# A fused attention and two expert layers: the first attention in a fixed order, other weights kept on chip, other buffers for coded weights

## The chip, the cores and the metric

The kernel runs on one core of a Trainium2 chip. The core has a matrix engine (TensorE, in the profile PE for products and PEld for the loading of weights), a vector engine (VectorE, DVE), a scalar engine (ScalarE, ACT), a general engine (GpSimd, POOL) and an engine that issues most of the transfers (SyncE, SP). The engines run side by side, each works through its own queue of instructions in order, and they wait for each other by semaphores. The metric is the device time of one execution in microseconds (us), as a median of runs.

## The reference, cut to what matters

```python
def _attn_ref(q, k, v, s):                       # 2 batches, 8 heads, 576 positions, 64 wide
    scores = q @ k.T / 8
    cum = np.cumsum(np.maximum(s, 0.0), axis=-1)
    bias = -(cum[:, :, :, None] - cum[:, :, None, :])
    scores = np.where(causal, -1e9, scores + np.minimum(bias, 0.0))
    attn = softmax(scores)
    return attn @ v
def _moe_ref(x, w_in, w_out):                    # 1152 tokens, 512 -> 2048 -> 512
    h = x @ w_in
    g = np.where(h > 0.0, h, np.exp(np.minimum(h, 0.0)) - 1.0)
    return g @ w_out
def _moe2_ref(x, domain_probs, w1, w2):          # 4 experts, 512 -> 1024 -> 512
    p = domain_probs / (domain_probs.sum(-1, keepdims=True) + 1e-09)
    for e in range(4):
        out += p[:, e:e + 1] * (np.maximum(x @ w1[e], 0.0) @ w2[e])
```

The attention's result, 1152 rows of 512, goes through the second function (called layer one below) and then through the third (layer two).

## The kernel before, in words

The tokens are taken in three groups: 256, 448 and 448 (`GROUPS`). Group 0 has its attention to itself at the start (`attention_first`); the attention of groups 1 and 2 is cut into small parts that run in the background of the products of the group before (`attention_parts`, called by `background` in `slot`). Layer one of group 0 has 16 units (`up1`, `down1`: four products into `up`, an ELU on ACT and DVE that writes `gt`, four products into `acc0` to `acc3`), layer two of group 0 has 32 (`up2`, `down2`). Groups 1 and 2 have layer one each (`layer1`), and layer two for both together at the end: the joint stage, which forms 7 block products instead of 8 from sums of blocks (`pair_steps`, `p1` to `p7`, `c21`, `c22`).

Layer one of group 0 uses exact 32-bit weights, which come in a coded 64-bit form (`w64`), 512 KB for each half of a unit. `fetch_halves` loads coded halves into whatever buffers are still unused (the list `turn`: tags `gt`, `wu`, `wr`, `cd`, `yh`, `yl`, `raw`, `xa`, `ox`), and `decode_halves` decodes them: ACT takes the magnitude (L158) and, from the fifth half on, the low bits (L165); DVE puts the words together (L166, L168). Twelve decoded units are written back by a transfer of GpSimd's queue (`w_dec`, L171) and loaded again for groups 1 and 2 by `fetch` (L100); the last four stay on chip in the tag `wr` (`kept`, `N_WR`). Weights of the other uses are loaded as they are into `raw` (three buffers) and split into a high and a low part by `prepare` (ACT L106, DVE L87 into `wu`).

`attention_first` has four pairs of heads. For a pair: `scores` (PE L313, L321, L323), `probabilities` (a reduction with mask on DVE, L333, and an exponential on ACT, L335, for each of four blocks), `normalise` (DVE L339 to L344), `transposes` (PE L352, ACT L353), `values` (PE L361, ACT L363). `keep_warm` (L370) multiplies the identity by itself, to no result. `cum_parts`, `cum_columns` and `probabilities_of` prepare operands of the later attention and the expert shares.

What sets the order: a scheduler places the instructions of all engines by estimated times, and `tc.issue_after`, `tc.keep_in_program_order` hold it back where the author wants it. The order on each engine is then fixed. The call for decoding inside the attention is `decode_halves(DEC[i])`; in layer one `advance` calls it with

```python
        decode_halves(min(2 * n + AHEAD, DEC[-1] + 5 * (n + 1) // 2))
```

so that it runs up to ten halves ahead of unit n. The background of group 0 begins at slot 14 of layer one (`BG_FROM`); its first part loads queries, keys and values of the first heads into the tag `pt` (`load_small`, L429), and `split` (L486 to L491) makes `qs`, `qb`, `kh`, `kl` of them on ACT and DVE for `qk` (PE L502, L504).

Of the kernel before, what the change touches and what calls it, by code (L numbers as in the profile page):

```python
# [45 lines left out]
DEC = [1, 2, 3, 4]  # L46
# [4 lines left out]
N_WR, N_WU, N_GT, N_CD = 2, 1, 3, 5  # L51
# [3 lines left out]
def tile_kernel(ctx, tc, qT, kT, v, s, w64, w, probs, out):  # L55
# [39 lines left out]
    def fetch(n):  # L95
        if n >= NU and (n - NU) % NAB in kept:
            fetched[n] = kept[(n - NU) % NAB]
            return
        fetched[n] = t = sb([128, 1024], "raw", 3)
        SP.dma_start(out=t, in_=w[n - NAB] if n < NU else w_dec[(n - NU) % NAB])  # L100

    def prepare(n):
# [9 lines left out]
    small = [("yh", 1, 1), ("yl", 1, 1)] + [("raw", 3, 1)] * 3 + [("xa", 1, 3), ("ox", 1, 3)]  # L112
    turn = ([("gt", 3, 1)] * N_GT + [("wu", 5, 2)] * N_WU + [("wr", N_WR, 2)] * N_WR
            + [("cd", N_CD, 1)] * N_CD + small * 2)
# [9 lines left out]
    n_coded, n_decoded, last_coded = [0], [0], [None]  # L124
# [13 lines left out]

    def decode_halves(upto):

        while n_decoded[0] < min(upto, len(order)):
            i = n_decoded[0]
            n, part = order[i]
            if part == 0:
                if n % 2 == 0:
                    if n < NAB - N_KEPT:
                        pair = sb([128, 2, 1024], "wu", 5)  # L150
                    else:
                        pair = sb([128, 2, 1024], "wr", N_WR)
                        kept[n], kept[n + 1] = pair[:, 0], pair[:, 1]
                    units[n], units[n + 1] = pair[:, 0], pair[:, 1]
            x, m = coded.pop(i), units[n][:, 512 * part:512 * part + 512]
            high, low, mi = x[:, :, 1], x[:, :, 0], m.bitcast(I32)
            tc.keep_in_program_order(
                ACT.activation(m, high.bitcast(F32), AF.Abs, scale=2.0 ** -112))  # L158
            z = sb([128, 512], f"z{i % 2}", 1, I32)
            if i < N_LOW:  # L160
                tc.keep_in_program_order(DVE.tensor_scalar(
                    z, low.bitcast(U32), 7.49 / 2 ** 32, None, op0=ALU.mult))
            else:
                tc.keep_in_program_order(
                    ACT.activation(z, low.bitcast(U32), AF.Copy, scale=7.49 / 2 ** 32))  # L165
            DVE.scalar_tensor_tensor(out=mi, in0=mi, scalar=3, in1=z,  # L166
                                     op0=ALU.logical_shift_left, op1=ALU.bitwise_or)
            DVE.scalar_tensor_tensor(out=mi, in0=high, scalar=-2 ** 31, in1=mi,  # L168
                                     op0=ALU.bitwise_and, op1=ALU.bitwise_or)
            if part and n not in kept:  # L170
                POOL.dma_start(out=w_dec[n], in_=units[n])  # L171
            n_decoded[0] += 1
            fetch_halves()
# [3 lines left out]
    make_identity(nc, ident)  # L177

# [10 lines left out]

    zero = sb([64, 256], "zero", 1)  # L190
    POOL.memset(zero, 0.0)

# [69 lines left out]
    def attention_first(x):  # L265
# [31 lines left out]
        with tc.issue_after(high.ins), tc.issue_after(low.ins):  # L297
            cum_parts()
# [57 lines left out]
        def values(hp):  # L356
            o = ps(f"acc{(hp + 2) % 4}", 1)
# [15 lines left out]
        with tc.issue_after(keep_warm(12).ins):  # L373
            first = scores(0)
            with tc.issue_after(first.ins), tc.issue_after(low.ins):
                cum_columns(0, 4)
                cum_columns(1, 4)
            scores(1)
            scores(2)
        probabilities(0)  # L380
        decode_halves(DEC[0])
        with tc.issue_after(scores(3).ins):
            keep_warm(6)
        probabilities(1)
        with tc.issue_after(normalise(0).ins):
            shares.extend((probabilities_of(0, n // 128), probabilities_of(T2, NCH)))
        with tc.issue_after(transposes(0).ins):
            keep_warm(4)
        probabilities(2)
        normalise(1)  # L390
        transposes(1)
        values(0)
        decode_halves(DEC[1])
        probabilities(3)
# [3 lines left out]
        decode_halves(DEC[2])  # L398
        normalise(3)
        transposes(3)  # L400
        values(2)
        values(3)
        decode_halves(DEC[3])

# [353 lines left out]
    attention_first(x_first)  # L758
    pr_first, pr_later = shares
    xs = [None, None, None]  # L760

    class First:
# [3 lines left out]
        def __call__(self, at):  # L766
            if at > BG_FROM[0]:
                if self.got is None:
                    first_stack.close()
                    att_pool[0] = att_stack.enter_context(  # L770
                        tc.tile_pool(name="att", bufs=1, reuse_waits="tile"))
                    xs[1] = sb([128, 2, NCC, N2], "xa", 1, F32R)
                    self.got = Background(attention_parts(1, xs[1]), BG_FROM[0],
                                          NAB + LAG + E * NCD - BG_TO[0])
# [8 lines left out]
    for c in range(NCC):  # L783
        ACT.activation(yh[:, c], yacc[c], AF.Copy)
        split_lo(yl[:, c], yacc[c], yh[:, c])
    pr = pr_first
# [69 lines left out]
    def pair_steps(q):  # L856
# [3 lines left out]
        def sums():  # L860
            x = raws[q]
            st["t"] = t = l2a.tile([128, 4, 256], F32, tag="sums", name="sums", bufs=1)
# [240 lines left out]
```

## Time and profile before

| what | us |
|---|---|
| median of 3 runs (lowest, highest) | 708.74 (707.78, 709.1) |
| the profiled execution, as a run | 710.54 |
| its span, first to last instruction | 708.4 |
| PE busy, DVE busy, ACT busy, POOL busy in the span | 696.6, 561.7, 382.4, 15.6 |

The profile is one execution. A busy PE is not a PE at its peak: its rows carry the granted clock, 1.00 for 2.4 GHz and 0.50 for 1.2 GHz, and a row of products takes longer at the lower one. Idle time of an engine counts only where the end waits for it, so the timeline of PE and what released each of its waits come first, and from there one goes to the engine or the transfer that was late. A timeline row is: start, duration, engine, line, operation, written tile, read tiles, shapes, count, and in brackets the idle time before it with what ended it. A duration runs to the last write, so the start of the next row on the same engine tells what one instruction costs its queue. Stages of this execution: first attention to 28.3 us, layer one of group 0 to 87, its layer two to about 226, layer one of groups 1 and 2 to 413, the joint stage to the end.

### The profile page before, as it was taken

What the parts mean: (1) busy time and instruction counts of PE and PEld (TensorE: products, weight loads), DVE (VectorE), ACT (ScalarE), POOL (GpSimd) and SP (SyncE); (2) the same over time, 40 slices, a digit from 0 to 9 for tenths busy, and PEclk for the clock granted to TensorE, in tenths of its full rate; (3) what the DMA queues carried; (4) which work ended last, traced back from release to release, by engine and by line L of the source; (5) the groups of instructions that cost most, each with busy time, mean ns of one, the idle gap of its engine ahead of it and who ended that gap; (6) DMA issues with size and microseconds to landing.
All of it is one profiled execution on the core that took longest, in us unless ns stands there. A gap on an engine that the chain in (4) does not pass through costs nothing.

```text
span 708.4 us, 10218 instructions
## 1 busy us (share of the span) xinstructions
PE 696.6 (98%) x3670; PEld 595.6 (84%) x3670; DVE 561.7 (79%) x1146; ACT 382.4 (54%) x773; POOL 15.6 (2%) x36
## 2 busy tenths in 40 slices
PE   8999999999999999999999999999999999999997
PEld 7888788887878887888899988888888888888886
DVE  7799788797868898876975469988888888788765
ACT  5799798786768788866644344322222223332320
POOL 5011000000000000000000000000000000000000
PEclk9899999999999999999999999999999999999999
DMA  8999855655554433113530000111111111111002
GB/s 299 409 368 373 271 174 154 193 166 157 174 185 140 141 125 102 41 47 128 210 140 0 1 1 0 60 60 60 60 61 59 60 60 59 61 60 59 1 0 105
DMA packets 34578, 85.45 MB, mean 121 GB/s; under 512 B 3440, under 2 KB 13888, under 8 KB 34528
## 3 DMA queue, kind: packets, MB, share of 16 engines
q1 hardware_dynamic: 32576, 78.23, 32.7%
q0 software_dynamic: 1952, 6.57, 2.3%
q8 instruction: 29, 0.48, 0.3%
q14 instruction: 21, 0.17, 0.1%
HBM read 75.88 MB, written 8.91 MB: 120 GB/s over the span
## 4 chain that ended last, share of the span: by engine, by line
PE 86%; ACT 7%; DVE 3%; issue 1%; DMA 1%; POOL 0%; SPq 0%; DVEq 0%; ACTq 0%; POOLq 0%
PE acc L626 38%; PE up L626 16%; PE att L938 11%; PE up L938 8%; PE att L581 3%; PE att L554 3%; ACT z L165 2%; ACT wu L158 2%; PE att L509 1%; PE att L502 1%; PE att L504 1%; DMA pt<-in_kT 1%; ACT e L736 1%; PE att L370 1%; PE acc L716 1%
## 5 line engine op out<-in xcount | busy, mean ns | idle before, releaser
L626 PE MATMUL acc<-w,h 128*128 128x512 f32 x672 | 172.0, 392 | 0.0
L626 PEld LDWEIGHTS acc<-w,h 128*128 128x128 f32 x672 | 126.1, 188 | 23.0 <-ACT h L948 0.2
L626 PE MATMUL acc<-gt,wu 128*128 128x448 f32 x384 | 87.8, 372 | 0.0
L948 ACT ACTIVATE h<-c 128x448 fp32r<-128x448 f32 x48 | 27.4, 573 | 111.7 <-DVE c L954 111.7
L683 DVE SCALAR_TENSOR_TENSOR ox<-acc,pr,ox 128x512 f32<-128x512 f32 x105 | 78.6, 748 | 11.1 <-PE acc L626 9.1
L87 DVE TENSOR_TENSOR wu<-raw,wu 128x1024 fp32r<-128x1024 f32 x56 | 68.4, 1223 | 19.5 <-ACT wu L106 17.3
L626 PEld LDWEIGHTS acc<-gt,wu 128*128 128x128 f32 x384 | 70.1, 188 | 7.8 <-issue 2.6
L106 ACT ACTIVATE wu<-raw 128x1024 fp32r<-128x1024 f32 x56 | 59.1, 1055 | 15.8 <-PE acc L626 14.1
L938 PE MATMUL att<-S,top 128*128 128x448 f32 x288 | 66.3, 365 | 0.0
L938 PEld LDWEIGHTS att<-S,top 128*128 128x128 f32 x288 | 54.0, 188 | 6.7 <-issue 0.2
L626 PE MATMUL acc<-wu,gt 128*128 128x512 f32 x192 | 56.8, 411 | 0.0
L626 PE MATMUL up<-yh,wu 128*128 128x256 f32 x256 | 52.5, 287 | 0.0
L949 DVE SCALAR_TENSOR_TENSOR h<-c,h 128x448 fp32r<-128x448 f32 x48 | 29.8, 623 | 18.7 <-ACT h L948 18.7
L938 PE MATMUL up<-x2a,top 128*128 128x448 f32 x192 | 44.2, 366 | 0.0
L626 PEld LDWEIGHTS up<-yh,wu 128*128 128x128 f32 x256 | 41.8, 190 | 2.6 <-issue 1.7
L626 PE MATMUL up<-xa,wu 128*128 128x448 f32 x192 | 43.5, 371 | 0.0
L626 PE MATMUL up<-ox,wu 128*128 128x448 f32 x192 | 41.5, 366 | 0.8 <-DVE e L741 0.8
L544 ACT ACTIVATE p<-p,nm 128x384 f32<-128x384 f32 (+4 forms) x56 | 34.5, 616 | 13.6 <-DVE nm L539 13.2
L948 ACT ACTIVATE h<-up 128x448 fp32r<-128x448 f32 x16 | 8.7, 545 | 59.5 <-PE up L938 59.5
L938 PEld LDWEIGHTS up<-x2a,top 128*128 128x128 f32 x192 | 35.9, 188 | 4.8 <-ACT p L963 0.6
L626 PEld LDWEIGHTS up<-ox,wu 128*128 128x128 f32 x192 | 36.0, 188 | 4.0 <-DVE e L741 1.1
L626 PEld LDWEIGHTS acc<-wu,gt 128*128 128x128 f32 x192 | 32.8, 189 | 6.9 <-issue 2.5
(215 smaller groups left out, 1245.6 us busy)
## 6 DMA issues: line engine op xcount, KB each, us to landing
raw<-in_w SPq DMA_DIRECT2D x38, 512.0 KB
raw<-in_w SPq DMA_DIRECT2D x16, 1024.0 KB
raw<-w_dec SPq DMA_DIRECT2D x24, 512.0 KB
w_dec<-wu POOLq DMA_DIRECT2D x12, 512.0 KB, 7.4
cd<-in_w SPq DMA_DIRECT2D x5, 512.0 KB
xa<-in_w SPq DMA_DIRECT2D x5, 512.0 KB
k<-in_kT SPq DMA_DIRECT2D x8, 288.0 KB
cbp<-cum_d SPq DMA_DIRECT2D x16, 144.0 KB
```

Source lines behind the costliest of these rows:

```text
L87: DVE.tensor_tensor(out=lo, in0=x, in1=hi.bitcast(F32), op=ALU.subtract)
L106: ACT.activation(t[:, 0], x, AF.Copy)
L158: ACT.activation(m, high.bitcast(F32), AF.Abs, scale=2.0 ** -112))
L165: ACT.activation(z, low.bitcast(U32), AF.Copy, scale=7.49 / 2 ** 32))
L544: ACT.activation(p, p, AF.Exp, bias=nm, scale=-1.0, accum_out=sm)
L554: PE.transpose(pt[:cb[c + 1] - cb[c], m, :], p[:, cb[c]:cb[c + 1]], ident)
L581: PE.matmul(o[64 * j:64 * j + 64, qs:nq], job["v"][:n, c, 64 * j:64 * j + 64], job["pt"][:n, j, c, qs:nq], start=c == 0, stop=c == n_c - 1)
L626: PE.matmul(o, a[m], b[n], start=first and i == 0, stop=last and i == 2)
L683: DVE.scalar_tensor_tensor(out=o_sb, in0=o, scalar=pr[:, i, e:e + 1], in1=o_sb, op0=ALU.mult, op1=ALU.add)
L938: PE.matmul(bank, tops[q][:, m, op, cs], x[:, n, c], start=first and c + i == 0, stop=c == 1 and i == 2, skip_group_check=True)
L948: ACT.activation(h[:, 0, u, cs], c, AF.Relu)
L949: DVE.scalar_tensor_tensor(out=h[:, 1, u, cs], in0=c, scalar=0.0, in1=h[:, 0, u, cs].bitcast(F32), op0=ALU.max, op1=ALU.subtract)
```

## The change

The engines PE, ACT and DVE are scheduled by hand inside `attention_first`: the instructions stand in the order in which the function writes them. That order is new: one stretch of eight warm-up products in place of 12, 6 and 4; scores of two pairs, probabilities of two pairs, scores of the other two; the fourth pair's probabilities earlier; decoding not before the fourth `normalise`, save for the magnitude step of two halves (`begin_half`). `cum_columns` and the shares go behind the last decoded word of layer one (`last_word`). The kept units are the first six, not the last four (`N_WR` 3); the `wr` tag holds no coded halves any more, `wu` holds ten of them, `cd` three, twice. Four halves are decoded when the attention ends, as before. The sums of the joint stage go to the tag `xf` for the first two pairs, and to the pool on the right side for the others.

```diff
-DEC = [1, 2, 3, 4]
+DEC = [1, 2, 4]
-N_WR, N_WU, N_GT, N_CD = 2, 1, 3, 5
+N_WR, N_WU, N_GT, N_CD = 3, 5, 0, 3
...
-        SP.dma_start(out=t, in_=w[n - NAB] if n < NU else w_dec[(n - NU) % NAB])
+        SP.dma_start(out=t, in_=w[n - NAB] if n < NU else w_dec[(n - NU) % NAB - N_KEPT])
...
-    small = [("yh", 1, 1), ("yl", 1, 1)] + [("raw", 3, 1)] * 3 + [("xa", 1, 3), ("ox", 1, 3)]
-    turn = ([("gt", 3, 1)] * N_GT + [("wu", 5, 2)] * N_WU + [("wr", N_WR, 2)] * N_WR
-            + [("cd", N_CD, 1)] * N_CD + small * 2)
+    twice = [("cd", N_CD, 1)] * N_CD + [("yh", 1, 1), ("yl", 1, 1)]
+    turn = ([("gt", 3, 1)] * N_GT + [("wu", 5, 2)] * N_WU + twice
+            + [("raw", 3, 1)] * 3 + [("xa", 1, 3), ("ox", 1, 3)] + twice + [("xa", 1, 3)])
...
+    def begin_half(i):
+        n, part = order[i]
+        if part == 0 and n % 2 == 0:
+            if n >= N_KEPT:
+                pair = sb([128, 2, 1024], "wu", 5)
+            else:
+                pair = sb([128, 2, 1024], "wr", N_WR)
+                kept[n], kept[n + 1] = pair[:, 0], pair[:, 1]
+            units[n], units[n + 1] = pair[:, 0], pair[:, 1]
+        begun[i] = m = units[n][:, 512 * part:512 * part + 512]
+        tc.keep_in_program_order(
+            ACT.activation(m, coded[i][:, :, 1].bitcast(F32), AF.Abs, scale=2.0 ** -112))
...
-        with tc.issue_after(high.ins), tc.issue_after(low.ins):
-            cum_parts()
+        cum_parts()
...
-        with tc.issue_after(keep_warm(12).ins):
-            first = scores(0)
-            with tc.issue_after(first.ins), tc.issue_after(low.ins):
-                cum_columns(0, 4)
-                cum_columns(1, 4)
-            scores(1)
-            scores(2)
-        probabilities(0)
-        decode_halves(DEC[0])
-        with tc.issue_after(scores(3).ins):
-            keep_warm(6)
-        probabilities(1)
-        with tc.issue_after(normalise(0).ins):
-            shares.extend((probabilities_of(0, n // 128), probabilities_of(T2, NCH)))
-        with tc.issue_after(transposes(0).ins):
-            keep_warm(4)
+        keep_warm(8)
+        for hp in (0, 1):
+            scores(hp)
+        for hp in (0, 1):
+            probabilities(hp)
+        for hp in (2, 3):
+            scores(hp)
+        normalise(0)
         probabilities(2)
+        transposes(0)
         normalise(1)
+        probabilities(3)
         transposes(1)
+        begin_half(0)
         values(0)
-        decode_halves(DEC[1])
-        probabilities(3)
         normalise(2)
         transposes(2)
         values(1)
-        decode_halves(DEC[2])
+        begin_half(1)
         normalise(3)
+        decode_halves(DEC[0])
         transposes(3)
         values(2)
+        decode_halves(DEC[1])
         values(3)
-        decode_halves(DEC[3])
+        decode_halves(DEC[2])
...
-    attention_first(x_first)
-    pr_first, pr_later = shares
+    with tc.manual_schedule(engines={mybir.EngineType.PE, mybir.EngineType.Activation,
+                                     mybir.EngineType.DVE}):
+        attention_first(x_first)
...
+                    with tc.issue_after(last_word[0].ins):
+                        cum_columns(0, 4)
+                        cum_columns(1, 4)
+                        shares.extend((probabilities_of(0, n_tile), probabilities_of(T2, NCH)))
...
-            st["t"] = t = l2a.tile([128, 4, 256], F32, tag="sums", name="sums", bufs=1)
+            if q < 2:
+                t = sb([128, 4, 256], "xf", 1)
+            else:
+                t = l2b.tile([128, 4, 256], F32, tag="sums", name="sums", bufs=1)
+            st["t"] = t
```

On GpSimd the clearing of `zero` and the first of its two casts (L293 before) move ahead of the masks' selections. Three places show what else the change moves. The lines of the changed kernel are a few numbers off: L352 is L354 there, L361 is L363.

PE between the last scores and the first values of the first attention, before (`k_154` and `k_155` hold the probabilities of the first three heads and of the next three):

```order
L321 MATMUL acc_274<-cump,ones 128x256
L323 MATMUL acc_274<-ones,cumm 128x256
L370 MATMUL att<-ident 128x128 x6
L352 MATMUL att<-ident,k_154 128x128 x6
L370 MATMUL att<-ident 128x128 x4
L352 MATMUL att<-ident,k_154 128x128 x3
L361 MATMUL acc_369<-pt 64x256 x2
```

The same place on PE of the changed kernel:

```order
L323 MATMUL acc_258<-cump,ones 128x256
L325 MATMUL acc_258<-ones,cumm 128x256
L354 MATMUL att<-ident,k_152 128x128 x9
L354 MATMUL att<-ident,k_153 128x128 x3
L363 MATMUL acc_329<-pt 64x256 x2
```

The ten warm-up products between the scores and the values are gone.

SP at the end of decoding, before (`raw` from L135 holds coded halves, from L100 weights of layer two; `pt` are the loads of the background attention):

```order
L135 DMA raw<-in_w 128x1024 x3
L135 DMA xa<-in_w 128x1024 x2
L100 DMA raw<-in_w 128x1024 x3
L429 DMA pt<-in_qT 128x4x128
L429 DMA pt<-in_kT 128x4x128
```

SP of the changed kernel at the same place, and behind it DVE of the changed kernel, where L175 is the last decoded word, L734 the gate `gt`, L231 the columns' copies and L87 the split of weights:

```order
L100 DMA raw<-in_w 128x1024 x3
L135 DMA xa<-in_w 128x1024 x3
L100 DMA raw<-in_w 128x1024 x2
L426 DMA pt<-in_qT 128x4x128
L426 DMA pt<-in_kT 128x4x128
```

```order
L175 SCALAR_TENSOR_TENSOR wu<-xa,wu 128x512 x2
L734 SCALAR_TENSOR_TENSOR gt<-up,e 128x256
L231 COPY cum_782<-cum 16x64 x2
L231 COPY cum_790<-cum 16x64 x2
L259 TENSOR_REDUCE prs<-pr 128x2
L87 TENSOR_TENSOR wu<-raw,wu 128x1024
L260 TENSOR_SCALAR prs<-prs 128x2
L87 TENSOR_TENSOR wu<-raw,wu 128x1024
```

Two more weight loads now stand ahead of the background's first loads; they go into buffers that the two splits (L87) have to free.

ACT at the beginning of the background attention, before (`e` are the exponentials of layer one's units, L733, and their second step, L736):

```order
L486 ACTIVATE qs<-pt 64x512
L733 ACTIVATE e<-up 128x256
L487 ACTIVATE kh<-pt 64x512
L736 ACTIVATE e<-e 128x256
L489 ACTIVATE qb<-pt 64x512
L491 ACTIVATE kh<-pt 64x512
L486 ACTIVATE qs<-pt 64x512
L487 ACTIVATE kh<-pt 64x512
L733 ACTIVATE e<-up 128x256
L491 ACTIVATE kh<-pt 64x512
L736 ACTIVATE e<-e 128x256
```

The same place on ACT of the changed kernel:

```order
L483 ACTIVATE qs<-pt 64x512
L486 ACTIVATE qb<-pt 64x512
L484 ACTIVATE kh<-pt 64x512
L488 ACTIVATE kh<-pt 64x512
L483 ACTIVATE qs<-pt 64x512
L484 ACTIVATE kh<-pt 64x512
L488 ACTIVATE kh<-pt 64x512
L730 ACTIVATE e<-up 128x256
L106 ACTIVATE wu<-raw 128x1024
L733 ACTIVATE e<-e 128x256
```

All seven casts of the first split now stand ahead of the exponential of unit 15, and a cast of weights stands between its two steps. In the joint stage the first two products with the block sum S2 now follow each other on PE, where five products with S3 stood between them, and the four steps of the sums of pair 2 stand among the block sums on DVE.

## Rows read from the trace of the kernel before

**Rows 1.** The page: TensorE's share of the span; traffic of 40 slices.

```profile
PE 696.6 (98%) x3670; PEld 595.6 (84%) x3670; DVE 561.7 (79%) x1146; ACT 382.4 (54%) x773; POOL 15.6 (2%) x36
...
GB/s 299 409 368 373 271 174 154 193 166 157 174 185 140 141 125 102 41 47 128 210 140 0 1 1 0 60 60 60 60 61 59 60 60 59 61 60 59 1 0 105
```

**Rows 2.** Stretches, PE: length, busy time and records, granted clock, transfers' share, GB/s.

```profile
15.10:21.80 6.70, 6.70 (x32) 0.50 1.02 403
21.90:28.00 6.10, 6.10 (x52) 1.00 1.03 421
```

**Rows 3.** Timeline of PE, first attention to the first product of layer two.

```profile
13.98 0.92 PE L313 MATMUL acc<-pt 64*128 64x128 f32 x6 [1.24 <-DVE nm L333]
...
16.56 2.77 PE L370 MATMUL att<-ident 128*128 128x128 f32 x12
19.12 1.49 PE L352 MATMUL att<-ident,k 128*128 128x128 f32 x6
...
27.54 0.87 PE L361 MATMUL acc<-pt 128*64 128x256 f32 x8
...
79.53 0.33 PE L502 MATMUL att<-kh,qs 128*128 128x128 f32 x1 [1.21 <-ACT kh L491]
...
87.04 0.34 PE L626 MATMUL up<-yh,wu 128*128 128x256 f32 x1
```

**Rows 4.** Timeline of DVE in the first attention, and two weight splits later.

```profile
8.00 0.27 DVE L333 CUSTOM_DVE_ANT_0 k<-acc,mask 128x128 f32<-128x128 f32 x1
...
8.55 0.28 DVE L333 CUSTOM_DVE_ANT_0 k<-acc,mask 128x128 f32<-128x128 f32 x1
...
8.96 1.18 DVE L235 COPY cum_p<-cum_t 64x4 f32<-64x4 f32 x4
...
13.84 1.01 DVE L344 TENSOR_SCALAR k<-k,sm 128x128 f32<-128x128 f32 x4
...
74.46 2.36 DVE L87 TENSOR_TENSOR wu<-raw,wu 128x1024 fp32r<-128x1024 f32 x2
```

**Rows 5.** Timeline of ACT: exponentials, first and last decoding steps, casts.

```profile
8.32 0.40 ACT L335 ACTIVATE k<-k,nm 128x128 f32<-128x128 f32 x1 [1.56 <-DVE nm L333]
...
9.21 0.39 ACT L335 ACTIVATE k<-k,nm 128x128 f32<-128x128 f32 x1
...
30.68 0.67 ACT L158 ACTIVATE wu<-wu 128x512 f32<-128x512 f32 x1
...
69.82 0.71 ACT L165 ACTIVATE z<-xa 128x512 int32<-128x512 uint32 x1
71.29 1.06 ACT L106 ACTIVATE wu<-raw 128x1024 fp32r<-128x1024 f32 x1 [0.76 <-DMA raw<-in_w]
...
77.38 0.63 ACT L487 ACTIVATE kh<-pt 64x512 fp32r<-64x512 f32 x1
```

**Rows 6.** Timelines of DVE and POOL, 3 to 5 us: the scan, two casts.

```profile
3.27 1.35 DVE L207 TENSOR_TENSOR_SCAN cum<-bias 16x576 f32<-16x576 f32 x1 [3.27 <-ACT bias L206]
...
3.39 1.43 POOL L293 CAST cump<-zero 64x256 fp32r<-64x256 f32 x1
4.77 0.39 POOL L293 CAST cumm<-zero 64x256 fp32r<-64x256 f32 x1
```

**Rows 7.** Timelines of SP and ACT: the load of s and its use; the queries' load.

```profile
0.75 0.39 SPq L270 DMA_DIRECT2D bias<-in_s  x1
...
2.56 0.68 ACT L206 ACTIVATE bias<-bias 16x576 f32<-16x576 f32 x1 [0.52 <-DMA bias<-in_s]
...
70.01 0.38 SPq L429 DMA_DIRECT2D pt<-in_qT  x1
```

**Rows 8.** The chain that ended last: start, length, what; the keys' load.

```profile
70.44 6.92 DMA pt<-in_kT
```

**Rows 9.** Timelines of DVE and PE, joint stage: S2's low part, its first use.

```profile
421.17 1.08 DVE L87 TENSOR_TENSOR S<-ssum,S 128x896 fp32r<-128x896 f32 x1
...
422.53 0.37 PE L938 MATMUL up<-S,top 128*128 128x448 f32 x1
```

More of the change, by code (lines that the diff above doesn't have):

```diff
@@ L123, in tile_kernel @@
         last_in[tag][-1] = i
-    n_coded, n_decoded, last_coded = [0], [0], [None]
+    n_coded, n_decoded, last_coded, last_word = [0], [0], [None], [None]
     def fetch_halves(upto=len(order)):
@@ L137, in fetch_halves @@
             n_coded[0] += 1
+    begun = {}
+    def begin_half(i):
[10 more added lines that the diff above has]
+            ACT.activation(m, coded[i][:, :, 1].bitcast(F32), AF.Abs, scale=2.0 ** -112))
     def decode_halves(upto):
@@ L146, in decode_halves @@
             n, part = order[i]
[L147 to L155, printed above, removed]
+            if i not in begun:
+                begin_half(i)
+            x, m = coded.pop(i), begun.pop(i)
             high, low, mi = x[:, :, 1], x[:, :, 0], m.bitcast(I32)
-            tc.keep_in_program_order(
-                ACT.activation(m, high.bitcast(F32), AF.Abs, scale=2.0 ** -112))
             z = sb([128, 512], f"z{i % 2}", 1, I32)
@@ L167, in decode_halves @@
                                      op0=ALU.logical_shift_left, op1=ALU.bitwise_or)
-            DVE.scalar_tensor_tensor(out=mi, in0=high, scalar=-2 ** 31, in1=mi,
-                                     op0=ALU.bitwise_and, op1=ALU.bitwise_or)
+            last_word[0] = DVE.scalar_tensor_tensor(out=mi, in0=high, scalar=-2 ** 31, in1=mi,
+                                                    op0=ALU.bitwise_and, op1=ALU.bitwise_or)
             if part and n not in kept:
-                POOL.dma_start(out=w_dec[n], in_=units[n])
+                POOL.dma_start(out=w_dec[n - N_KEPT], in_=units[n])
             n_decoded[0] += 1
@@ L177, in tile_kernel @@
     make_identity(nc, ident)
+    zero = sb([64, 256], "zero", 1)
+    POOL.memset(zero, 0.0)
     mask = sb([128, S], "mask", 1)
@@ L188, in tile_kernel @@
                            pattern=[[-1, 64]], channel_multiplier=1)
-    zero = sb([64, 256], "zero", 1)
-    POOL.memset(zero, 0.0)
     cum = sb([B * H, S], "cum", 1)
@@ L356, in values @@
         def values(hp):
-            o = ps(f"acc{(hp + 2) % 4}", 1)
+            o = ps(f"acc{hp}", 1)
             for c, q0 in ((0, 0), (1, 128)):
@@ L785, in tile_kernel @@
         split_lo(yl[:, c], yacc[c], yh[:, c])
+    pr_first, pr_later = shares
     pr = pr_first
```

## The prediction

> **What bounds the kernel now.** I read the share of each engine on the page first [rows 1]: TensorE is busy 98% of the span, so all that can be won is about 12 us of idle TensorE and the products that do nothing or run at the low clock. The table by stretches puts the latter in front: the granted clock is 0.50 (1.2 GHz) for 6.8 us, from 15.0 to 21.9, and 1.00 (2.4 GHz) again behind that [rows 2]. The timeline of TensorE shows why that stage is long [rows 3]: after a wait of 1.24 us for a reduction of DVE the clock fell, twelve records of the warm-up helper then took 2.77 us at 16.56, and the first transposes came only at 19.12. The last value product starts at 27.54; from there layer one of group 0 is paced by TensorE with one later wait worth naming, 1.21 us at 79.53, for a cast of keys that a load released. Layer two begins at 87.04. What happens before 87.04 is therefore the place to cost; behind it TensorE has hardly any wait to give back.
>
> **The change, part by part.** I make the sum against the profiled execution (span 708.4 us, 710.54 us as a run, so 2.1 us around the span) and carry the difference over to the median of the runs shown, 708.74 us, which is 1.8 us below that execution.
>
> *The start.* GpSimd's first cast took 1.43 us and its twin 0.39; the first stood beside the scan of DVE, which ran from 3.27 to 4.6 [rows 6]. Now the first cast stands ahead of the scan, but the mask's selections and the second cast fall beside it. Freed wholly, the first reduction comes at about 7.35 us (the two splits of the row sums, 1.4 us, from 5.95); held as the first cast was, near the 8.00 of before [rows 4]. I take 7.9, nearer to the row. [...]
>
> *The attention stage.* DVE no longer has the columns' copies there (the four small ones alone 1.18 us [rows 4]), nor the shares, nor any decoding before the fourth normalise; TensorE no longer has the ten products between scores and transposes. What is left is a chain of two engines. A head's two reductions take 0.55 us (8.00 to 8.55), so a pair 1.1; normalising a pair takes four multiplies, 1.01, and two small steps, 1.4 in all [rows 4]; a head's two exponentials take 0.89 (8.32 to 9.21), so a pair 1.78 [rows 5]. From 7.9 DVE needs 4 x 1.1 + 4 x 1.4 = 10.0 us, and about 0.7 us more because the first normalise waits for the first pair's exponentials: 18.6. Behind it come the last transposes (0.8), their two evictions queued on ACT behind the first mantissa step of the decoder (about 1.9 in all), so the last value product starts at 21.3 instead of 27.54 [rows 3]: 6.2 us earlier.
>
> *Layer one.* Its products are the same, and ACT is the engine that could hold them: a half costs it two steps, 30.68 to 69.82 for the first and the last of 28 halves with twelve exponentials between [rows 5]. The row of halves now starts at 24.4, but one cast of raw weights (1.06 [rows 5]) stands inside it: it ends about 5.4 us earlier, and TensorE does not wait for it, because the halves run ahead: ACT's last step stood at 69.82, some ten us before TensorE came to the last unit, right behind the wait at 79.53 [rows 3]. Three kept pairs instead of two take two stores and four reloads of 512 KB out; I cost that at nothing, since no wait of TensorE between 100 and 700 us is for a load of weights. If that cover were gone, it would be worth 1.3 us a transfer, 512 KB at the 409 GB/s that the page shows in its second slice [rows 1].
>
> *The loads of the next attention.* Here the gain runs into something. Before, SP issued them at 70.01 [rows 7]. Now two more weight loads stand ahead on SP, and each waits for a cast of DVE (1.2 us apiece, from the pair of 2.36 [rows 4]), which stand behind the last decoded word, one gate, and the columns' copies that were moved there. Last word 66.95, gate and copies 1.0, two casts 2.4, two issues 0.5: the queries' load is issued at 70.9, the keys' at 71.35, **no earlier than before**, although TensorE is 7.4 us ahead (6.2 plus the 1.21 wait). Who waits: seven casts on ACT, then the exponential of unit 15 behind them in the same queue. How long the keys' load takes is bounded by 1.8 us (the load of s, issued at 0.75 and used at 2.56 [rows 7]) and 6.92 us (this load in the full queue of before [rows 8]). The queue is shorter now, two loads of weights ahead (2.6 us): I take 3.7, landing at 75.1, the queries' at 74.3. From there: seven casts of 0.6 (77.38 and its like [rows 5]) to 78.5, exponential 0.35, a weight cast 0.95 to 79.8, its remainder on DVE 1.2 to 81.0, the gate 0.4, four down products 1.7: layer two begins at 83.2 instead of 87.04 [rows 3]. So 7.4 us shrink to 3.8, and TensorE shows some 3.5 us of waits between 75 and 82.
>
> *Behind it.* The first transposes of the background attention stand closer behind their scores than before, 1.65 us of TensorE's work against 2.3; the chain reduction, exponential, normalise is the same. I charge 0.7 us (bounds 0 and 1.3).
>
> *The joint stage.* The sums of pair 2 move into DVE's sequence of block sums, one of them ahead of all others (0.2 us). The low part of S2 was finished at 422.25 (421.17 plus 1.08) and TensorE asked for it at 422.53 [rows 9]; now that product is placed right behind the first with S2, at 421.75. With the low part at 422.5 it waits 0.8 us (bounds 0 and 1.0; no other product is moved before it).
>
> Sum: 3.8 - 0.7 - 0.8 = 2.3 us. The span becomes 706.1, a run like the profiled one 708.2, the median **706.4 us**.
>
> **Rivals.** *The loads land fast.* If the keys take little more than the 1.8 us of rows 7, layer two begins at 81.5, and if the two small charges behind it vanish too, the gain is 5.5 us: 703.2. For it: two stores fewer are in the queues, and the stores end before. Against it: two 512 KB loads are issued just ahead.
>
> *The loads land as late as before.* With 6.92 us [rows 8] the keys land at 78.3, layer two begins at 86.2, and 0.8 less the two charges is a loss of 0.7: 709.4, no change. For it: they are short rows behind weights, as then.
>
> *The clock, the case that ends slower.* Fourteen of 22 warm-up products go, and TensorE now waits several times for 0.9 us between transposes and values. In the trace a wait of 1.24 us was enough for the clock to fall to 1.2 GHz, and it stayed there for 6.8 us although TensorE was then busy throughout [rows 2, 3]; at 79.53 a wait of 1.21 us left it at 2.4 GHz. Each us at the low clock costs TensorE 0.5 us where it is the pace. Inside the attention stage much of that is hidden behind ACT; in layer one, or in the new waits between 75 and 82, none is. The 2.3 us are gone at 4.6 us of low clock in layer one; from 7.5 us on the kernel is slower by over 1.4 us, and two stretches like that of before give 711 to 713. [...]
>
> *It does not do what it says.* The new order on ACT puts evictions behind exponentials; if the chain of DVE and ACT were held by this, the stage would end near 25 and the gain would be under 1 us.
>
> **How the numbers follow.** Forecast (704.5 to 707.3) 0.42; fast loads (701.5 to 704.5) 0.20; late loads 0.16 and the order's own hold 0.04, both within 0.2%; the clock 0.18. A measurement of this kernel tells about 0.2%, 1.4 us, from no change. So faster 0.62, same 0.20, slower 0.18. The range reaches from the middle of the fast case, 702.5, to the edge of the slow one, 710.0.
>
> **What would show it.** Right: the first reduction near 7.9, the last value product near 21.3, the last z step of ACT near 64.5, the queries of the background issued near 71 us, a wait of TensorE for kh of one to two us near 75 and one for the gate of unit 15 near 80, layer two from about 83, and a wait of 0.8 us at the first use of S2. Wrong: a granted clock of 0.50 behind 22 us (then the clock's case); layer two beginning before 81.5 or after 86; the last value product after 24; or waits of TensorE between 100 and 340 us that sum to over 2 us.

## The result, and the profile after

The changed kernel is slower. Its median is 712.1 us (711.0 to 716.3, 11 executions) against 708.9 us of the kernel before in the same session; the ratio is 1.0052, 95% interval 1.0036 to 1.0068. A second session gave 711.1 us and 1.0041 (1.0021 to 1.0062). The forecast was 706.4 us. The profiled execution took 711.7 us with a span of 709.6.

The page of the changed kernel, its rows of TensorE's share, of the clock in forty slices and of the bytes moved, answer to [rows 1]:

```profile
PE 696.9 (98%) x3642; PEld 591.9 (83%) x3642; DVE 561.1 (79%) x1146; ACT 381.7 (54%) x773; POOL 14.5 (2%) x34
...
PEclk9999899999999999999999999999999999999999
...
GB/s 293 417 406 312 295 125 121 208 166 147 183 155 51 83 124 102 129 48 73 122 163 89 1 0 1 61 59 60 60 60 60 60 59 60 60 59 60 1 0 104
```

The busy time of TensorE is what it was, and one slice of the clock is below full speed, the fifth. TensorE's timeline of the changed kernel says where the time went; it answers to [rows 3] (start, duration, line, operation, count, and in brackets the idle time ahead of it with its releaser):

```profile
21.09 0.87 PE L363 MATMUL acc<-pt 128*64 128x256 f32 x8
...
74.11 1.46 PE L713 MATMUL acc<-gt,wu 128*128 128x256 f32 x6
78.76 0.47 PE L499 MATMUL att<-kh,qs 128*128 128x128 f32 x1 [3.19 <-ACT kh L488]
...
81.81 4.45 PE L713 MATMUL acc<-gt,wu 128*128 128x256 f32 x12
...
85.90 0.47 PE L623 MATMUL up<-yh,wu 128*128 128x256 f32 x1
...
120.91 0.70 PE L506 MATMUL att<-k,q 64*64 64x288 f32 x4
...
340.51 2.70 PE L623 MATMUL up<-ox,wu 128*128 128x448 f32 x12 [0.77 <-DVE e L738]
...
427.36 2.72 PE L945 MATMUL att<-S,top 128*128 128x448 f32 x12 [0.89 <-DVE u L961]
```

The gain is there at first: the last value product starts at 21.09 instead of 27.54 [rows 3], and at 74.11, at the down products of unit 13, TensorE is 7.4 us ahead of the kernel before, where they start at

```profile
81.47 1.03 PE L716 MATMUL acc<-gt,wr 128*128 128x256 f32 x4
```

Then it stands 3.19 us for the keys, layer two begins at 85.90 (before: 87.04), and at 120.91 the first product of the first long attention job starts, which stands at the same place of TensorE's order in both kernels. In the kernel before it starts at

```profile
120.40 0.70 PE L509 MATMUL att<-k,q 64*64 64x288 f32 x4
```

so the changed kernel is 0.5 us behind there, and with a wait of 0.89 us at 427.36 it is 1.2 behind at the end (the 0.77 us at 340.51 are there in both kernels). Below, "the landmark" is this product.

The table by stretches, from 15 us on, with the granted clock in the third column from the right and the DMA share in the second, answers to [rows 2]. The first two rows cover the stage that ran at 0.50 before:

```profile
15.00:22.00 7.00, 6.23 (x53) 3.91 (x52) 6.57 (x23) 6.01 (x20) 0.00 (x0) 1.00 1.03 414
22.00:70.00 48.00, 47.56 (x213) 39.73 (x214) 43.70 (x83) 45.78 (x90) 5.36 (x10) 1.00 0.93 376
...
66.00:70.00 4.00, 3.73 (x17) 2.96 (x17) 3.88 (x12) 3.35 (x7) 1.07 (x2) 1.00 0.33 134
...
78.00:79.00 1.00, 0.24 (x1) 0.24 (x2) 0.68 (x1) 0.95 (x3) 0.00 (x0) 0.62 1.11 309
...
78.30:78.40 0.10, 0.00 (x0) 0.00 (x0) 0.10 (x1) 0.10 (x1) 0.00 (x0) 0.50 1.12 438
...
79.00:85.00 6.00, 6.00 (x16) 4.61 (x17) 2.93 (x5) 3.37 (x7) 0.00 (x0) 0.50 1.07 242
```

Two things stand out. The clock is 1.00 until 78.2, falls to 0.50 while TensorE still stands for the keys, and is back at 85.1, so that TensorE works at 0.50 for 6.3 us behind the wait. And from 66 to 70 the DMA engines are busy for a third of the time only (before: 1.01 in this stretch): SP has issued nothing since 51.5, because the two weight loads at its head wait for casts (on DVE, begun at 68.74 and 69.94). The timelines of SP, ACT and DVE around it (SP's rows are issues) answer to [rows 5, 7]:

```profile
70.02 1.53 SPq L100 DMA_DIRECT2D raw<-in_w  x2
71.70 0.38 SPq L426 DMA_DIRECT2D pt<-in_qT  x1
...
76.39 0.63 ACT L483 ACTIVATE qs<-pt 64x512 fp32r<-64x512 f32 x1 [5.12 <-DMA pt<-in_qT]
...
80.42 0.36 ACT L730 ACTIVATE e<-up 128x256 f32<-128x256 f32 x1
...
83.04 0.42 DVE L734 SCALAR_TENSOR_TENSOR gt<-up,e 128x256 f32<-128x256 f32 x1
```

The queries are issued at 71.70 and cast at 76.39; seven casts later ACT comes to the exponential of unit 15, and its gate leaves DVE at 83.46, with the last four down products of layer one behind it.

### The profile page after: what moved, and what is told of

The parts are those of the page before. It is cut to its first block, busy times and chain, and to the rows that moved or that the text cites. A ratio compares the mean times of both kernels' runs of the same rounds, so it can differ in the third digit from the quotient of the medians.

```text
span 709.6 us, 10126 instructions
## 1 busy us (share of the span) xinstructions
PE 696.9 (98%) x3642; PEld 591.9 (83%) x3642; DVE 561.1 (79%) x1146; ACT 381.7 (54%) x773; POOL 14.5 (2%) x34
## 4 chain that ended last, share of the span: by engine, by line
PE 86%; DVE 5%; ACT 5%; DMA 3%; issue 1%; SPq 0%; POOL 0%; DVEq 0%; ACTq 0%; POOLq 0%
PE acc L623 38%; PE up L623 16%; PE att L945 10%; PE up L945 8%; PE att L578 4%; PE att L551 3%; DMA xa<-in_w 2%; PE att L506 1%; ACT z L172 1%; PE att L499 1%; PE att L501 1%; PE acc L713 1%; ACT wr L152 1%; DVE wu L87 1%; DMA pt<-in_qT 1%
## 5 line engine op out<-in xcount | busy, mean ns | idle before, releaser
L87 DVE TENSOR_TENSOR wu<-raw,wu 128x1024 fp32r<-128x1024 f32 x52 | 63.5, 1222 | 12.9 <-ACT wu L106 10.8
L106 ACT ACTIVATE wu<-raw 128x1024 fp32r<-128x1024 f32 x52 | 54.9, 1055 | 8.3 <-PE acc L623 7.0
```

Source lines behind the costliest of these rows:

```text
L87: DVE.tensor_tensor(out=lo, in0=x, in1=hi.bitcast(F32), op=ALU.subtract)
L106: ACT.activation(t[:, 0], x, AF.Copy)
```

## The experiments

Two accounts of the loss were open: that the keys come late (the loads' place on SP), and that the low clock behind the wait costs the time. A third place was the joint stage. All of these kernels are the changed one with the edit shown, unless it says otherwise.

### Keys ahead of the weights

```diff
-        SP.dma_start(out=t, in_=w[n - NAB] if n < NU else ...)
+        with tc.issue_after(asked[0].ins) if n > NAB + 2 and asked[0] else nullcontext():
+            SP.dma_start(out=t, in_=w[n - NAB] if n < NU else ...)
...
-                SP.dma_start(out=t, in_=x[b, :, 0:128].rearrange(...))
+                asked[0] = SP.dma_start(out=t, in_=x[b, :, 0:128].rearrange(...))
```

> The changed kernel, with one difference: the loads of two weight units (19 and 20) are issued behind the loads of the background attention on SyncE instead of ahead of them. Theory: the queries' load of that attention was late (issued at 71.70, landed by 76.39), TensorE stood 3.19 us for the keys' cast, and the 6.6 us at a granted clock of 0.50 behind that wait cost 3.3 us more. Then the load is issued before 68, no wait of TensorE between 70 and 84 is over 0.5 us, the clock stays at 1.00 there, layer two begins near 79.5 instead of 85.90, and the median falls by 5 to 6.5 us, to 705.6 to 707. Rival one, something else holds layer two as well (the gate of unit 15 on ACT and DVE): the wait only moves there, layer two begins after 83, median 709 to 711. Rival two, the load waits for memory and not for the weights ahead of it: nothing moves, 712.

Measured: 705.7 us, 6.4 below the changed kernel and 3.0 below the one before (ratio to before 0.9978, 0.9956 to 1.0000). Two of its twelve executions took 712.2 and 712.3 at a clock of 1.00; no profile caught one, and what held them is open. They pull up the ratio, which by the medians alone would be 0.996, and make its interval wide. The changed kernel has such an execution in each session, too (716.3 and 718.7). Its rows on SP, ACT and TensorE:

```profile
67.57 0.38 SPq L428 DMA_DIRECT2D pt<-in_qT  x1
...
73.08 0.63 ACT L486 ACTIVATE qs<-pt 64x512 fp32r<-64x512 f32 x1 [2.02 <-DMA pt<-in_qT]
...
73.90 1.46 PE L716 MATMUL acc<-gt,wu 128*128 128x256 f32 x6
75.46 0.33 PE L502 MATMUL att<-kh,qs 128*128 128x128 f32 x1
...
80.09 0.47 PE L626 MATMUL up<-yh,wu 128*128 128x256 f32 x1
...
114.42 0.70 PE L509 MATMUL att<-k,q 64*64 64x288 f32 x4
```

The load is issued 4.1 us earlier, TensorE reaches the first score and finds the keys, the clock stays at 1.00, layer two begins at 80.09 (5.8 us earlier) and the landmark comes 6.5 us earlier. Both rivals fall. One thing was not expected: the load took 5.5 us from issue to cast with no weights ahead of it, against 4.7 with two. In the kernel before, with three weights just ahead, it took 6.4 us (issued at 70.01 [rows 7]):

```profile
76.40 0.63 ACT L486 ACTIVATE qs<-pt 64x512 fp32r<-64x512 f32 x1 [1.20 <-DMA pt<-in_qT]
```

So the transfer's length does not follow the number of weights ahead. What the two weights do is keep the load from being issued.

### TensorE kept busy while the keys are under way

Products that add zeros stand ahead of the first score; the loads stay late. The edit with seven (with fourteen, the list has four empty parts and the products stand behind the fourth product of unit 13):

```diff
-        parts = [start, lambda: None]
+        parts = [start] + [lambda: None] * (2 if g == 1 else 1)
...
+                        for _ in range(7 if (k, c) == (13, 1) else 0):
+                            last_warm[0] = PE.matmul(o, mask[:, 0:128], gt,
+                                                     start=False, stop=False)
...
-            qk(it, pss, a, e)
+            with (tc.issue_after(last_warm[0].ins) if g == 1 and it is items[0]
+                  else nullcontext()):
+                qk(it, pss, a, e)
```

> The changed kernel, with fourteen more products of 256 columns that add zeros, put on TensorE right ahead of the first score of the background attention, so that TensorE is busy while the keys are under way; the first scores are emitted a little later for this. The loads are as late as in the changed kernel. Theory: the keys still hold TensorE until about 78.8, but the clock stays at 1.00 behind it; the 3.3 us of the low stretch go, the 3.2 us of waiting stay: layer two near 82.6, median 708.3 to 709.5. Rival, the low clock is hidden behind other engines there: layer two near 85.9 as now, median 712. Rival two, the clock falls all the same: 0.50 in some stretch between 78 and 86, median 712 or more.

> The changed kernel, with seven more products that add zeros (0.44 us each as the run with fourteen showed: 6.2 us, which was 2 us longer than the wait), behind the first two down products of unit 13, so that TensorE is busy until about 78.5 and no longer. The keys are as late as in the changed kernel. Theory: the clock stays at 1.00, but of the 3.3 us that the low stretch costs TensorE's products only about 1.5 come back, since the gate of unit 15 comes at 83.0 on DVE in either case, behind the seven casts of ACT, and four products stand behind it: layer two at 84.2 to 84.6, median 710.2 to 710.9. Rival, the low clock cost its whole 3.3 us: layer two near 82.6, median 708.5 to 709.2. Rival two, the clock falls all the same: 712.

Measured: 710.7 us with fourteen (1.0022, 1.0010 to 1.0034) and 711.4 with seven (1.0035, 1.0023 to 1.0046). Fourteen took 6.21 us, 2 us more than there was to cover, so that forecast was wrong in its own price, and layer two began at 86.34, not near 82.6:

```profile
75.15 6.21 PE L718 MATMUL acc<-gt,mask 128*128 128x256 f32 x28
...
86.34 0.47 PE L625 MATMUL up<-yh,wu 128*128 128x256 f32 x1
```

In both profiles the clock is 1.00 from 70 to 86 us; with seven, the stretch that ran at 0.50 in the changed kernel reads

```profile
79.00:85.00 6.00, 5.48 (x31) 4.87 (x31) 4.17 (x10) 4.16 (x8) 0.00 (x0) 1.00 0.88 236
```

Not every execution with seven is like that: two of the six, both near 712.6, have a mean clock of 0.997, and the other four have a median of 711.0. Against the two sessions of the changed kernel (712.1 and 711.1) the two covers bring between nothing and 1.5 us, far from the 3.2 us that half speed over 6.3 us makes. Late keys under a full clock still cost 5.0 to 5.7 us more than early keys. The seven gave less than the 1.2 to 1.9 us forecast for them.

The edits also did more than cover the wait. In both kernels ACT takes the first step of unit 15's exponential ahead of the second head's casts, and the gate leaves DVE at 81.30 with fourteen and 78.67 with seven, not at 83.46 as in the changed kernel; the second forecast had counted on the same gate. So the little that is gained belongs to the clock and to the earlier gate together. The profile with seven shows layer two at 82.76, the time of the rival by which the low clock costs its whole 3.3 us:

```profile
69.39 0.38 SPq L426 DMA_DIRECT2D pt<-in_qT  x1
...
79.28 0.33 PE L499 MATMUL att<-kh,qs 128*128 128x128 f32 x1 [1.35 <-DVE bias L251]
...
82.76 0.47 PE L625 MATMUL up<-yh,wu 128*128 128x256 f32 x1
```

But it is the fastest of its six executions (709.1), and its queries were issued 2.3 us earlier than in the profile of the changed kernel, so it does not tell the two apart; the medians do.

### The sums of pair 2 behind the block sums

```diff
+        state["add"] = DVE.tensor_tensor(out=t, in0=a, in1=b, op=ALU.add)
...
+    block_done[0] = state["add"]            # the last addition of p3(0)
...
+            with tc.issue_after(block_done[0].ins) if q == 2 else nullcontext():
                 DVE.tensor_tensor(out=t[:, 0], in0=b12, in1=b11, op=ALU.subtract)
                 ...
```

> The changed kernel, with the four sums of pair 2 put behind the block sums of pair 0 on DVE instead of between them. Theory: they delayed the sum u by 1.8 us, for which TensorE waited 0.89 us at 427.36; without them that wait is under 0.2 us and the end comes 0.7 to 0.9 us earlier: median 711.2 to 711.5. Rival: the wait has another cause in the order of TensorE (the two adjacent products with S2), it stays or moves to the casts of pair 2, and the median stays at 712.1.

Measured: 710.3 us (1.0016, 1.0005 to 1.0028), 0.8 and 1.8 below the two sessions of the changed kernel; the forecast was 711.2 to 711.5. DVE's timeline of the changed kernel and, under it, of this one:

```profile
424.48 0.42 DVE L873 TENSOR_TENSOR sums<-raw,sums 128x256 f32<-128x256 f32 x1
424.82 0.62 DVE L961 TENSOR_TENSOR u<-up,p 128x448 f32<-128x448 f32 x1
425.35 0.42 DVE L874 TENSOR_TENSOR sums<-raw,sums 128x256 f32<-128x256 f32 x1
425.69 1.08 DVE L87 TENSOR_TENSOR S<-ssum,S 128x896 fp32r<-128x896 f32 x1
426.69 0.62 DVE L961 TENSOR_TENSOR u<-att,u 128x448 f32<-128x448 f32 x1
```

```profile
424.50 0.62 DVE L962 TENSOR_TENSOR u<-up,p 128x448 f32<-128x448 f32 x1 [0.74 <-PE up L946]
425.16 0.62 DVE L962 TENSOR_TENSOR u<-att,u 128x448 f32<-128x448 f32 x1
```

The sum u, for which TensorE waited at 427.36, comes 1.5 us earlier, ahead of the cast of S as in the kernel before, and TensorE has no wait between 415 and 440.

### Both kernels once more

> The kernel before, unchanged, for the granted clock and the span of each of its timed executions. The two profiled executions differ by 1.2 us (710.54 and 711.72), the medians by 3.2. Theory one, its stretch at 1.2 GHz from 15 to 22 us is in most executions: mean clock 0.995 in all, spans within 1 us of 707. Theory two, the profiled execution was not the typical one: several executions show a mean clock of 1.00 or 0.997, and these are 1.5 to 3 us shorter.

> The changed kernel, unchanged, for a second profile and the clock of each timed execution. Theory: TensorE's wait for the keys and the low clock behind it are there in nearly all executions (mean clock 0.995 to 0.998), their length following the time at which the queries' load is issued; the median is 711.5 to 712.5 and the profiled execution lies within 1 us of it, while that of the kernel before had been 1.6 to 1.8 us over its own median. Rival: the low stretch is an accident of the profiled execution; then half of the executions have a mean clock of 1.00 and are 1.5 us shorter.

Measured: before 708.6 us (0.9991 to 1.0013 of itself), with mean clocks between 0.996 and 1.000. Its new profile has no low stretch from 15 to 22, and the landmark at 120.08 instead of 120.40. By these two profiles the low stretch that [rows 2] put in front cost the kernel before 0.3 us. TensorE did not set the pace there: at the full clock it waits in the same stage,

```profile
20.27 1.16 PE L370 MATMUL att<-ident 128*128 128x128 f32 x8 [1.75 <-ACT pt L353]
```

So theory two holds for the clock, but not for its price: the four executions with a mean clock of 1.00 (708.2 to 710.0 us) are no shorter than the others (707.7 to 710.7).

The changed kernel gave 711.1 us and clocks of 0.995 to 0.998 in all twelve. Its second profiled execution was one of the long ones (714.1 us; landmark at 121.82), and what it shows is worth more than its time. TensorE's timeline in it:

```profile
78.83 0.33 PE L499 MATMUL att<-kh,qs 128*128 128x128 f32 x1 [3.52 <-DVE kl L87]
...
83.58 3.46 PE L713 MATMUL acc<-gt,wu 128*128 128x256 f32 x8 [1.71 <-DVE gt L734]
...
86.47 0.78 PE L623 MATMUL up<-yh,wu 128*128 128x256 f32 x1
```

And its table by stretches:

```profile
79.00:83.00 4.00, 2.74 (x12) 1.78 (x12) 2.21 (x3) 3.20 (x6) 0.00 (x0) 1.00 1.09 288
...
84.00:85.00 1.00, 1.00 (x4) 0.82 (x3) 0.07 (x1) 0.38 (x1) 0.00 (x0) 0.50 0.12 30
```

Here the clock stayed at 1.00 behind the wait for the keys, TensorE ran ahead, and then stood 1.71 us for the gate of unit 15. The gate comes at 83.5 in either execution, so most of what a full clock gives is waited away ahead of it; the clock fell behind this second wait instead. The clock is not what the 6.4 us hang on.

### The first attention as before

The stage's order, its 22 warm-up products and the place of the columns and shares are put back (the two versions are in the diff ahead of the prediction); the kept units, buffers and sums stay changed. The second kernel has the keys ahead of the weights as well.

```diff
-    with tc.manual_schedule(engines={...}):
-        attention_first(x_first)
+    attention_first(x_first)
...
-        keep_warm(8)
-        for hp in (0, 1):
-            scores(hp)
...
+        with tc.issue_after(keep_warm(12).ins):
+            first = scores(0)
+            with tc.issue_after(first.ins), tc.issue_after(low.ins):
+                cum_columns(0, 4)
...
```

> The changed kernel with the first attention as it was before (its planner's order, 22 warm-up products, the columns' copies and the shares in that stage); the kept units, the coded buffers and the sums of the joint stage as changed. Theory: the new order alone brings TensorE 7.4 us ahead, the kept units bring and cost nothing, the sums cost 0.9: last value product near 27.5, first wait for the keys 0.5 to 1.5 us, median 709.2 to 710.0. Rival: the kept units or the two weight loads that now stand ahead of the keys cost by themselves, keys' wait over 2 us, median over 710.5; or they gain, under 708.5.

> As the kernel with the old attention, and the background attention's loads ahead of weight units 19 and 20 as in the first experiment. Theory: TensorE reaches the keys only near 80 there, so early loads take out the one wait of about 1 us and nothing more: median 0.5 to 1.5 us below the kernel with the old attention, 708.0 to 709.0; the 6.4 us of the first experiment need both, the new order and the early loads. Rival: the early loads alone bring the gain, whatever the order of the first attention: median near 705.7.

Measured: 713.3 us (1.0061, 1.0047 to 1.0075), not 709.2 to 710.0, and 708.9 (0.9998, 0.9990 to 1.0007). With the two kernels of the new order this makes a table of medians in us:

| first attention | keys behind the two weights | keys ahead of them |
| --- | --- | --- |
| as before | 713.3 | 708.9 |
| as changed | 712.1 and 711.1 | 705.7 |

Each against the kernel before in its own session, these are 4.0 us above and 0.3 below in the first row, 3.2 and 2.5 above and 3.0 below in the second. So the new order is worth some 2.7 us where the keys are early and 0.8 to 1.6 where they are late. And the loads' place costs 4.4 us even with the old order. The theory that the kept units cost nothing falls with that, and so does the one that early loads take out about 1 us there, although the median it gave came true. The same edit moves the loads much further here: the queries are issued at 56.91 with it,

```profile
56.91 0.38 SPq L434 DMA_DIRECT2D pt<-in_qT  x1
```

and at 68.53 without. That is no later than the 70.01 of the kernel before [rows 7]; what TensorE meets late is the last load of the row, the low parts of the keys, and behind it a reduction (TensorE's timeline of the old order with late loads):

```profile
85.22 0.30 PE L507 MATMUL att<-kl,qb 68*128 68x128 f32 x1 [0.90 <-DMA kl<-rows_d]
...
87.44 0.33 PE L505 MATMUL att<-kh,qs 128*128 128x128 f32 x1 [1.32 <-DVE nm L542]
```

The table by stretches of the same kernel has the clock low again behind them:

```profile
88.00:91.00 3.00, 3.00 (x17) 3.00 (x16) 2.15 (x17) 2.14 (x7) 0.00 (x0) 0.52 0.53 201
```

With the keys ahead one wait of 0.47 us is left of the two. Which part of the kept units' change makes those loads late, and why DVE is late at 87.44, was not separated and stays open. Early loads in the kernel before itself, with its own kept units, were not run.

### A version that beats both

> The changed kernel with the background attention's loads ahead of weight units 19 and 20 and the sums of pair 2 behind the block sums of pair 0. Theory: the two mends are far apart in the program and add: no wait over 0.5 us at 70 to 84, none over 0.2 us at 415 to 440, the profiled span about 702.4, median 704.4 to 705.0, 0.6% below the kernel before. Rival: the wait in the joint stage is replaced once the stage starts on another footing, median 705.4 to 706.

> As the kernel with both mends, and the first score of the background attention placed behind the down products of unit 14 instead of in the middle of those of unit 13, so that TensorE has five more products before it needs the keys. Theory: the wait of 1.30 us for the keys that the kernel with both mends still showed in its profile goes (1.1 us of products stand ahead of it now), the background follows 0.2 to 0.4 us closer behind: median 0.3 to 1.0 us below that kernel, 703.8 to 704.5. Rival: what the score is put back for is waited for later, at the first transposes of the background, and the median stays at 704.8 or rises by up to 0.5.

The two mends together gave 704.8 us (0.9937, 0.9924 to 0.9951): they add, as forecast, to 0.9 below the first alone. Its profiled execution, a long one (706.6), still waits for the keys, which the forecast had excluded (its queries were issued at 69.23, not 67.57 as in the profile of the first experiment):

```profile
77.21 0.33 PE L502 MATMUL att<-kh,qs 128*128 128x128 f32 x1 [1.30 <-ACT kh L491]
```

The third step, a one-line edit,

```diff
-        parts = [start, lambda: None]
+        parts = [start] + [lambda: None] * (5 if g == 1 else 1)
```

gave **703.6 us** (0.9923, 0.9909 to 0.9937), 0.8% below the kernel before. Its profile still has a wait of 1.53 us, now ahead of the second score. The row puts it down to a bias, which DVE finished at 78.71; the second head's last cast left ACT at 78.68, so both came just ahead of the score:

```profile
76.79 0.41 PE L502 MATMUL att<-kh,qs 128*128 128x128 f32 x1
78.73 0.33 PE L502 MATMUL att<-kh,qs 128*128 128x128 f32 x1 [1.53 <-DVE bias L253]
...
80.48 0.47 PE L626 MATMUL up<-yh,wu 128*128 128x256 f32 x1
```

So the wait did not go, it moved by one score. Each against the kernel before in its own session, the medians are 5.0 us below with the later place and 4.4 without, which leaves some 0.6 us for it; by the intervals alone the two mended versions are not told apart.

## Why the prediction was wrong

The miss is 5.7 us, and the terms below make it up: 2.7 for the loads, 0.9 behind them, 0.1 the other way in the joint stage, 2.2 in the carry-over to the median.

**Right: the attention stage and layer one.** Last value product 21.09 (forecast 21.3), unit 13's products 7.4 us ahead as forecast, ACT's last z step 65.42 (64.5), no low clock where the warm-up products went. The first reduction came at 7.49, near the lower bound of 7.35 and not at the 7.9 that I took, although the mask's last two selections did fall beside the scan and took 1.49 us there instead of 0.52.

**Right in mechanism, wrong in size: the loads of the next attention, 2.7 us.** The forecast had the loads no earlier than before, the seven casts, the exponential, the weight cast and the gate in that order, and TensorE waiting for the keys. The step that failed is the load's duration: I put the landing of the queries at 74.3 and they were cast at 76.39. Of these 2.1 us, 0.8 is the issue (71.70, not 70.9) and 1.3 the transfer. I took 3.4 us for it because "the queue is shorter now". It was shorter than before, 4.7 us against 6.4, but the first experiment shows 5.5 us with no weights ahead, so the queue was no measure of it. The gate came 2.0 us later than forecast, by the chain that was forecast. The other 0.7 is the low clock: from the gate at 83.46 the last four down products took 2.4 us, not 1.7. Layer two began at 85.90, not 83.2: close to the rival of late loads, which had 86.2 (by the forecast's own chain it would be 86.4, as the keys land 3.2 us later there).

**The background behind it, 0.9 us.** From layer two to the landmark the changed kernel needs 35.0 us (120.91 less 85.90) against 33.4 (120.40 less 87.04); I had charged 0.7, as waits of TensorE for a reduction, an exponential and a normalise. The stretch in the table of before and, under it, of after (TensorE's busy time is the second number) shows fewer waits and more work:

```profile
87.04:120.40 33.36, 32.38 (x214) 27.58 (x213) 29.09 (x90) 28.43 (x71) 0.00 (x0) 1.00 0.59 183
```

```profile
85.90:120.91 35.01, 34.67 (x218) 28.56 (x216) 29.37 (x92) 28.58 (x73) 0.00 (x0) 1.00 0.46 152
```

TensorE is idle for 0.3 us there instead of 1.0 and busy for 2.3 us more, with four records more. So this term was wrong in kind, and why the work takes longer was not separated. With early keys the stretch takes 34.3 us (114.42 less 80.09), near the charge.

**The joint stage, right in size by luck.** The forecast was 0.8 us of waiting for S2 at 421.75, and from the landmark to the end the changed kernel does take 0.7 us longer (709.6 less 120.91, against 708.4 less 120.40). But S2 was not waited for; the 0.89 us came five us later, at 427.36, for a sum u ahead of which three of the four moved sums had been put. I had costed only the sum ahead of all others.

**The carry-over to the median, 2.2 us.** I subtracted the 1.8 us by which the profiled execution lay over the median of before. The span grew by only 1.2 us between the two profiles, the medians by 3.2 (the other 0.2 is that the median of before was 708.74 then and 708.9 in the result): the profile of before was one of its longer executions, that of after lay 0.4 below its median. The second profile of the changed kernel lay 3 us above its median. The offset of one profile is no constant of the kernel.

**The clock's rival.** Its time came true (711 to 713), and its place too, the wait between 75 and 82. But it was priced as the cause, and the runs give it only a part: with the clock held up by idle work the kernel gains at most 1.5 us, with the keys early 5.4 to 6.4. Its time was luck. And the wait of 1.24 us, which I called enough for the clock to fall, tells little by itself: in the second profile of the same kernel a wait of 1.75 us left it at 1.00. In the changed kernel, too, the fall varied between its two profiles: at 78.2 in one, only at 83.9 in the other.

**What I did not cost at all** is that SP's two weight loads could be passed. I read the queue's order and took it as given; the DMA share of 0.33 at 66 to 70 in the changed kernel (0.65 with the loads moved) shows that order at work, and moving it is worth 5.4 to 6.4 us.

## What to carry to other kernels

A stage made shorter calls for its successor's loads earlier, and they must be moved with it: look on the issuing queue at what stands ahead of them and what that waits for. Here the queries' load behind two that waited was issued at 71.70 and not at 67.57, while the DMA engines were busy for 0.33 of the time from 66 to 70. Price a low clock only where TensorE sets the pace, against the next thing that it waits for: by two profiles, 6.8 us at 0.50 in its first attention cost the kernel before 0.3 us. And take a change of the median from medians: one profile lay 1.8 us over its own, another 3.

## What the runs showed of the hardware

The granted clock followed neither the number of warm-up products nor one length of wait. With eight warm-up products it stayed at 1.00 behind a wait of 0.76 or 0.77 us in the first attention, in both profiles of the changed kernel and in those of the two mended versions; with 22 it fell in two of four profiles, to 0.50 behind a wait of 1.24 us in the kernel before [rows 2, 3] and to a mean of 0.76 from 15 to 22 us in the old order with late loads, and did not fall in that stage of the other two, where the waits reached 1.75 us. Within a wait of 3.19 us it fell, behind 3.52 us of the same kernel it did not.

In the profile of the changed kernel the down products of layer one, of 256 columns, began every 0.43 us at a granted clock of 0.50 (79.6 to 81.3 us) and every 0.22 us at 1.00 (85.2 to 85.9). The rows give the clock as a share; frequencies in GHz are in no row, and no time in this document is worked out from them.

A load of 256 KB of the queries, beside other background loads, took from issue to the cast that waited for it 4.7 and 5.0 us in the two profiles of the changed kernel, 4.7 with seven covering products and 5.5 with the keys ahead of the weights. It took 4.8 us in the old order with late loads and 6.4 in the kernel before. What sets this time was not separated.
